# 20 instead of 21 matmuls per feature block of the first FFN products, with the sums on VectorE and the copies on ScalarE

## The chip, the cores and the metric

One core of one Trainium2 chip. The metric is the device time of one execution in microseconds (us), as the median of several. Ratios between kernels are the mean time of one kernel's fast runs over the mean of the other's fast runs of the same rounds, so they are not quite the ratio of the medians quoted beside them. Names in the profile: PE is TensorE (PEld its weight loads), DVE is VectorE, ACT is ScalarE, POOL is GpSimd, SP is SyncE, and SPq is SyncE's queue of DMA issues. PSUM is the memory that the matmuls here write to, SBUF the one that they read from. L511 is line 511 of the kernel in question.

## The reference

```python
# q, k, v: (8, 8, 576, 64); w1, w2, w3: (512, 768); w_out: (768, 512); all computed in fp32
scores = (q @ k.transpose(0, 1, 3, 2)) / sqrt(64)
attn = (scores * Dmat) @ v                    # Dmat: gamma ** (row - col) below the diagonal, else 0
x = attn.transpose(0, 2, 1, 3).reshape(4608, 512)
h = maximum(maximum(x @ w1, x @ w2), x @ w3)  # first products
out = h @ w_out                               # second products
```

## The kernel before

The kernel works in nine tiles of 512 tokens, each of four chunks of 128. The first tile uses plain products while the weights are still being converted. From the second tile on, the first products are bilinear: a unit (one of three weights, two blocks of 128 features, 512 tokens, 512 inputs) is a 2 x 2 x 2 block product made with 7 products instead of 8. Each of the 7 is two matmuls of 128 x 128 by 256 columns, since the inner dimension of a half is 256.

```python
def up(t, h, fp, i):                      # cut
    x = ps_x.tile([P, NH], FP32, ...)     # NH = 256 columns
    product(1, x, True);  p1 = kept("p1", x)      # kept: ScalarE copies x to SBUF
    y = ps_y.tile(...)
    product(2, y, True);  vector.tensor_tensor(c11, y, p1, op=add)
    product(6, x, False); u2 = kept("u2", x)      # adds to the same bank after the copy
    z = ps_y.tile(...)
    product(7, z, True);  p7 = kept("p7", z)
    product(5, x, False); vector.tensor_tensor(c22, x, p7, op=add)
    product(4, z, False); vector.tensor_tensor(c21, z, u2, op=add)
    product(3, x, False)                          # then maxima into h
```

The retention (scores, masks, values, states) of the next tile is done in steps between units. Each step puts its instructions on the engines at once.

```python
opool = ctx.enter_context(tc.tile_pool(name="opool", bufs=2))
def store(r, c, osb, ...):
    nc.sync.dma_start(block..., osb...)           # same queue as all loads
def total(r, c, src, others):
    osb = opool.tile([P, NM, DM // 2], FP32, tag="osb", name="osb")
    for m, o in enumerate(others):
        nc.vector.tensor_tensor(osb[:, m, :], src[m], o[:], op=ALU.add)
    store(r, c, osb)
# retention steps of a pair of chunks a, b; m counts the parts of a tile
at(m, (keep, a), (transposes, a), (load, a + 2))
at(m + 1, (transposes, b), (decay_values, b))
at(m + 2, (scores, a), (scores, b), (load, b + 2))
at(m + 4, (decay_values, a + 2))
at(m + 5, (values, [a, b], [b, a + 2]))
```

## Time and profile before

| | before |
|---|---|
| time, median of 3 runs | 798.76 us (798.38 to 799.25) |
| span of the profiled run | 796.0 us |
| busy: TensorE / VectorE / ScalarE / GpSimd | 785.0 / 417.6 / 174.4 / 139.9 us |
| waits of TensorE on other engines and loads | 7.5 us, 6.2 of them in the first 30 us |
| one steady tile (from first second-product to the next tile's) | 84.4 to 85.3 us, the last 75.7 us (it has less retention) |

The table says that TensorE is the bound and hardly ever waits. The lines, and how they are read, are in the prediction below.

### The profile page before, as it was taken

The page shows a single profiled execution, that of the slowest core. Times are in us where ns is not written, and L with a number is a line of the kernel's source. Part 1 is how long each engine was busy: PE and PEld are TensorE (multiplying, and loading weights), DVE is VectorE, ACT ScalarE, POOL GpSimd, SP SyncE. Part 2 cuts the span into 40 slices and gives each one's busy share as a digit, 9 for nine tenths or more (in the row PEclk, how much of TensorE's full clock was granted, in tenths as well). Part 3 has the DMA queues.
Part 4 walks back from the last instruction along what each step waited for, and adds up shares of the span by engine and source line. Part 5 has one row for each costly group of instructions (what it writes and reads, how often), then busy time and mean ns, then how long its engine had stood idle before and what let it go on. Part 6 is the DMA issues. An engine that isn't in the chain of part 4 may idle for free.

```text
span 796.0 us, 13774 instructions
## 1 busy us (share of the span) xinstructions
PE 785.0 (99%) x5172; PEld 643.0 (81%) x5172; DVE 417.6 (52%) x833; ACT 174.4 (22%) x402; POOL 139.9 (18%) x158
## 2 busy tenths in 40 slices
PE   8899999999999999999999999999999999999998
PEld 7445456888888888888888888888888888888887
DVE  2898979664454534364535354544545343642441
ACT  2664632111111111111111111111111111112111
POOL 3110108511210130112111121112111201110000
DMA  9995643333333323332233423333333332001001
GB/s 212 233 230 127 173 91 100 57 55 57 89 58 57 58 75 61 64 58 60 63 56 55 89 59 57 57 57 90 58 55 57 78 68 54 1 14 40 1 1 53
DMA packets 236930, 59.27 MB, mean 74 GB/s; under 512 B 217920, under 2 KB 235584, under 8 KB 236864
## 3 DMA queue, kind: packets, MB, share of 16 engines
q1 hardware_dynamic: 236432, 58.14, 33.9%
q8 instruction: 40, 0.66, 0.4%
q10 hardware_dynamic: 432, 0.27, 0.1%
q14 instruction: 26, 0.21, 0.1%
HBM read 48.89 MB, written 9.44 MB: 73 GB/s over the span
## 4 chain that ended last, share of the span: by engine, by line
PE 95%; SPq 2%; DMA 1%; issue 0%; ACT 0%; DVE 0%; ACTq 0%
PE x L511 32%; PE z L511 15%; PE dx L383 11%; PE up L573 8%; PE y L511 8%; PE dz L383 5%; PE s L204 4%; PE o L257 4%; PE dy L383 3%; PE down L562 2%; PE o L270 2%; PE kv L224 2%; SPq L172 1%; DMA kraw<-in_k_dram 1%; SPq L327 0%; DMA out_dram<-osb 0%
## 5 line engine op out<-in xcount | busy, mean ns | idle before, releaser
L511 PE MATMUL x<-S,T 128*128 128x256 f32 x576 | 148.0, 379 | 0.6 <-ACT p L516 0.6
L511 PEld LDWEIGHTS x<-S,T 128*128 128x128 f32 x576 | 109.0, 190 | 16.4 <-ACT p L516 1.0
L361 POOL TENSOR_TENSOR H<-h 128x256 f32<-128x256 f32 x24 | 21.0, 873 | 320.9 <-DVE h L554 320.9
L511 PE MATMUL x<-xT,w 128*128 128x256 f32 x288 | 76.1, 387 | 0.0
L511 PE MATMUL x<-S,w 128*128 128x256 f32 x288 | 74.4, 381 | 0.7 <-DVE h L541 0.7
L511 PE MATMUL z<-xT,T 128*128 128x256 f32 x288 | 73.9, 379 | 0.0
L511 PE MATMUL y<-xT,w 128*128 128x256 f32 x288 | 73.9, 379 | 0.0
L511 PE MATMUL z<-S,w 128*128 128x256 f32 x288 | 73.9, 379 | 0.0
L541 DVE TENSOR_TENSOR tmp<-x,p 128x256 f32<-128x256 f32 x48 | 20.4, 425 | 100.2 <-PE x L511 100.2
L516 ACT COPY p<-x 128x256 f32<-128x256 f32 x72 | 26.8, 372 | 192.1 <-PE x L511 192.1
L286 DVE TENSOR_TENSOR xT<-o,gq 128x512 f32<-128x512 f32 (+1 forms) x40 | 23.6, 633 | 84.6 <-PE o L270 84.6
L573 PE MATMUL up<-xT,w 128*128 128x512 f32 x144 | 63.5, 596 | 0.5 <-DVE xT L286 0.5
L511 PEld LDWEIGHTS x<-S,w 128*128 128x128 f32 x288 | 49.4, 189 | 14.2 <-issue 1.3
L511 PEld LDWEIGHTS z<-S,w 128*128 128x128 f32 x288 | 54.7, 190 | 7.4
L511 PEld LDWEIGHTS y<-xT,w 128*128 128x128 f32 x288 | 54.7, 190 | 7.4
L511 PEld LDWEIGHTS x<-xT,w 128*128 128x128 f32 x288 | 53.0, 190 | 9.6 <-issue 1.5
L511 PEld LDWEIGHTS z<-xT,T 128*128 128x128 f32 x288 | 54.2, 189 | 7.9
L573 PEld LDWEIGHTS up<-xT,w 128*128 128x128 f32 x144 | 26.8, 190 | 32.3 <-issue 29.8
L207 DVE TENSOR_TENSOR st<-s,causal 128x512 f32<-128x512 f32 x72 | 45.0, 684 | 11.6 <-PE s L204 10.7
L176 POOL TENSOR_TENSOR vd<-vraw,gk 128x512 f32<-128x512 f32 x36 | 38.8, 1077 | 62.1 <-DMA vraw<-in_v_dram 62.1
L516 ACT COPY u<-x 128x256 f32<-128x256 f32 x72 | 26.8, 372 | 100.1 <-PE x L511 91.7
L383 PE MATMUL dx<-To,H 128*128 128x256 f32 x192 | 44.8, 383 | 0.0
(95 smaller groups left out, 1061.8 us busy)
## 6 DMA issues: line engine op xcount, KB each, us to landing
bits<-in_moe_w_dram SPq DMA_DIRECT2D x36, 256.0 KB, 5.1
out_dram<-osb SPq DMA_DIRECT2D x35, 256.0 KB, 2.1
kraw<-in_k_dram SPq DMA_DIRECT2D x32, 256.0 KB, 3.0
vraw<-in_v_dram SPq DMA_DIRECT2D x32, 256.0 KB, 3.5
qraw<-in_q_dram SPq DMA_DIRECT2D x464, 16.0 KB, 1.8
kxraw<-in_k_dram SPq DMA_DIRECT2D x464, 16.0 KB, 1.8
bits<-in_moe_w_out_dram SPq DMA_DIRECT2D x6, 512.0 KB, 4.5
qraw<-in_q_dram SPq DMA_DIRECT2D x6, 256.0 KB, 4.9
```

Source lines behind the costliest of these rows:

```text
L176: nc.gpsimd.tensor_tensor(t[:], raws.pop(("v", g))[:], gk[:].unsqueeze(2).to_broadcast([C, H, D]), op=ALU.mult)
L204: nc.tensor.matmul(s[j][:, p, :], lhsT=kT[r, p, :], rhs=qT[r, p, :], start=True, stop=True)
L207: nc.vector.tensor_tensor(st[:, j], s[j][:], masks[start_of(g)][:].unsqueeze(1).to_broadcast([C, NP, C]), op=ALU.mult)
L224: nc.tensor.matmul(kvs[g][half(h % 2), h // 2, :], lhsT=kr[r:, h, :], rhs=vds[g][r:, h, :], start=True, stop=True)
L257: nc.tensor.matmul(o[n % 2][half(c), m, n // 2, :], lhsT=vds[g][:, h, :], rhs=sts[g][:, h % 2, h // 2, :], start=m == 0 and n < 2, stop=be ...
L286: nc.vector.tensor_tensor(xT[t][:, b::2, i * C:(i + len(chunks)) * C].rearrange("p u (m c) -> p u m c", c=C), o[b][:].rearrange("p m u c - ...
L361: chores.append(lambda: (pool(s3, a11, a21, op=ALU.subtract), pool(s4, a12, s2, op=ALU.subtract)))
L383: nc.tensor.matmul(out[m], lhsT=hS[n](fp)[:, m * P:(m + 1) * P], rhs=late["T"][n][:, fp, :], start=first and fp == 0 and (m == 0 or last a ...
L511: nc.tensor.matmul(out[:], lhsT=w[:, d * P:(d + 1) * P], rhs=xS[t][n][:, d, :], start=first and d == 0, stop=d == 1, skip_group_check=True)
L516: nc.scalar.copy(c[:], src[:])
L541: nc.vector.tensor_tensor(c22, x[:], p7[:], op=ALU.add)
L573: nc.tensor.matmul(ps[:], lhsT=w_sb[i, fb][:, dc * P:(dc + 1) * P], rhs=xT[t][:, dc, :], start=(dc == 0), stop=(dc == NDC - 1))
```

## The change

The intent: one block of 128 features for all three weights is now made with 20 matmuls of 256 columns, where the 2 x 2 x 2 scheme needs 21. Partial sums build up in five PSUM chains (A to E). ScalarE copies 14 intermediate states of a block into a ring of 20 SBUF buffers, and VectorE joins them with 14 additions and maxima. Sums of x and of the weights all go to VectorE. Retention's VectorE operations and its loads no longer go out at once: they are queued (`soon`), and one is taken after every second product. In the second tile two of six blocks stay plain, to cover the making of the weight sums.

```diff
+PRODUCTS = """E a11 b12, E a14 b42, B s15 n5, A a22 b21, C s3 b23, B s19 b41, A s10 b32, C a13 b31, B s6 n2, A s13 b22,
+              C a11 b11, B s14 n1, A s11 n4, D s7 b43, B a23 n6, A s20 b33, D s16 b13, B a21 n3, A a21 n8, A a24 n7"""
...
-                raws[n, g] = raw.tile([P, NP, C // 32, 32], FP32, tag=n, name=n + "raw", bufs=3 if n == "q" else 2)
+                raws[n, g] = raw.tile([P, NP, C // 32, 32], FP32, tag=n, name=n + "raw", bufs=2)
...
+    def soon(step):
+        if spread:
+            urgent.append(step)
+        else:
+            step()
...
-            s1, s2, s3, s4 = (spool.tile([P, 2, NH], FP32, tag=f"S{n}", name=f"S{n}") for n in (1, 2, 3, 4))
-            nc.vector.tensor_tensor(s1[:], a21, a22, op=ALU.add)
...
+            for n, line in enumerate(X_SUMS):          # 13 sums of x, all on VectorE
+                soon(partial(step, n, *line))
...
+        def after(step):
+            if step not in ("E1", "E2", "C2", "C3", "A6", "B5"):
+                t = of[step] = ppool.tile([P, NH], FP32, tag="part", name="part")
+                nc.scalar.copy(t[:], ps[step[0]][:])
+            for out, ins, op in JOINS.get(step, ()):
...
+            nc.tensor.matmul(ps[chain][:], lhsT=factor(w, fb), rhs=xS[t][x], start=n == 1, stop=ends, ...)
+            after(f"{chain}{n}")
...
+        plain = (2, 3) if t == 1 else ()
...
-            at(m, (keep, a), (transposes, a), (load, a + 2))
-            at(m + 1, (transposes, b), (decay_values, b))
-            at(m + 2, (scores, a), (scores, b), (load, b + 2))
+            at(m, (keep, a), (transposes, b), (decay_values, b))
+            if a == 2 * CPT:
+                at(m, (load, a + 2))
+            at(m, (load, b + 2))
+            at(m + 2, (scores, a), (scores, b))
             at(m + 4, (decay_values, a + 2))
-            at(m + 5, (values, [a, b], [b, a + 2]))
+            at(m + 5, (values, [a, b], [b, a + 2]), (transposes, a + 2), (load, a + 4))
```

The cuts leave out the sums of the weights, the joins' table, the smaller buffer counts for the loads of k and v, and a first warm-up loop that is merged into another.

## The prediction

> **What bounds the kernel now.** I read the page's first table, then TensorE's waits, then a stretch of the timeline, because the sum of waits tells whether anything but TensorE's own work is worth removing.
>
> The page, busy time of each engine and the chain that ended last:
>
> ```profile
> PE 785.0 (99%) x5172; PEld 643.0 (81%) x5172; DVE 417.6 (52%) x833; ACT 174.4 (22%) x402; POOL 139.9 (18%) x158
> ...
> PE 95%; SPq 2%; DMA 1%; issue 0%; ACT 0%; DVE 0%; ACTq 0%
> ```
>
> TensorE (PE) is busy in 785.0 of 796.0 us and carries 95% of the chain. A busy PE need not be a full one, so the waits of its own instructions are needed (us in total, times, longest):
>
> ```profile
> PE kt L194 <- DMA kraw<-in_k_dram: 3.9, 2, 2.7
> PE warm L120 <- POOL ident masks.py:199: 1.4, 1, 1.4
> PE x L511 <- DVE h L541: 0.7, 1, 0.7
> PE x L511 <- ACT p L516: 0.6, 1, 0.6
> ```
>
> All seven rows of its waits come to 7.5 us, 5.3 of them before the first product. So only two things change the time: less TensorE work, or new waits. The price of the work is in the timeline, as start, duration, engine, line:
>
> ```profile
> 402.10 1.03 PE L511 MATMUL x<-xT,w 128*128 128x256 f32 x4
> ...
> 402.96 1.03 PE L511 MATMUL y<-xT,w 128*128 128x256 f32 x4
> 403.16 0.37 ACT L516 COPY p<-x 128x256 f32<-128x256 f32 x1 [3.03 <-PE x L511]
> ...
> 403.61 0.84 PEld L511 LDWEIGHTS x<-S,T 128*128 128x128 f32 x4
> 403.82 1.03 PE L511 MATMUL x<-S,T 128*128 128x256 f32 x4
> ```
>
> Each row is one product of two matmuls, recorded as four passes (every fp32 matmul of the program leaves two records). The reader should take the distance between starts, not the durations: from 400.37 to 413.32 fifteen products take 12.95 us, so a product costs 0.863 us and a 256-column matmul **0.432 us**. For 512 columns the chain of waits has
>
> ```profile
> 79.01 13.74 PE up L573 x32
> ```
>
> 32 passes in 13.74 us, so **0.859 us** per matmul: the plain product pays the same per column, and splitting columns in half is free.
>
> **What the Trainium skill says.** (1) "TensorE: Matmul & The Clock Gate", Back-to-back issue gap, gives N/2.4 + 2.5 ns warm, 109 ns for 256 columns. The pitch here is 216 ns per recorded pass, twice that; I use the trace. (2) "PSUM — Partial Sum Buffer", The four PSUM rules, says a synchronised read in the middle of an accumulation group is allowed, and its Specifications say VectorE may take only one tensor input from PSUM. The rows above agree with the first: ScalarE copies x at 403.16 and the next product adds to the same x at 403.82. Both together are why the change needs ScalarE copies. (3) "SBUF — State Buffer", SBUF: two separate sides, says a VectorE operation with two SBUF inputs and a GpSimd operation that reads SBUF lock each other out of a shared port pair. The trace agrees (mean ns of one):
>
> ```profile
> L295 DVE TENSOR_TENSOR S<-S,xT 128x512 f32<-128x512 f32 x8 | 13.1, 1631 | 0.3
> L294 DVE TENSOR_TENSOR S<-xT 128x512 f32<-128x512 f32 x8 | 5.5, 693 | 0.3
> ```
>
> The same addition takes 1631 ns instead of 693 where GpSimd works on its own S. (4) "Perfetto Trace Analysis", Optimizing Scalar/DVE Operations, says about half of a profiled duration overlaps the next instruction. In part:
>
> ```profile
> 139.10 0.42 DVE L545 TENSOR_TENSOR tmp<-z,u 128x256 f32<-128x256 f32 x1 [0.37 <-PE z L511]
> 139.44 0.41 DVE L547 TENSOR_TENSOR h<-h,tmp 128x256 f32<-128x256 f32 x1
> ...
> 149.12 0.42 DVE L343 TENSOR_TENSOR To<-w_out 128x256 f32<-128x256 f32 x1
> 149.58 0.43 DVE L344 TENSOR_TENSOR To<-w_out,To 128x256 f32<-128x256 f32 x1
> ```
>
> Independent VectorE operations start 0.34 us apart, and one that reads the result just before it starts 0.46 us after it.
>
> **The change part by part.** The order of instructions of both kernels gives exact counts.
>
> TensorE. Before: 8 token tiles x 9 units x 14 = 1008 matmuls of 256 columns. After: 46 blocks of 128 features x 20 = 920, and 24 more plain 512-column matmuls, because the second tile does two of its six blocks plainly while VectorE makes weight sums. Removed: 88 x 0.432 = 38.0 us. Added: 24 x 0.859 = 20.6 us. **Net -17.4 us**, all on the path. Second products (336 matmuls), first tile and retention keep their counts. The two warm-up loops become one; that is before data arrives, and I give it 0. Floor: 798.8 - 17.4 = **781.4 us**. The 2% line is 0.98 x 798.76 = 782.8, so 1.4 us of new waits decides the class.
>
> ScalarE. Before, 216 kept copies plus 24 to h; after, 644 kept copies, 14 per block. At 0.372 us that is 89 us out and 240 in: 174 to about 335 us, 43%. Inside a block 14 x 0.372 = 5.2 us of the 8.6 us that its 20 products take. The critical distance: the order leaves two products (0.863 us) between two steps of chain A or B, the same as now between x and x. In the rows above the copy ends at 403.53, the weight load starts at 403.61 and the matmul at 403.82, so the slack is some 0.1 to 0.2 us if ScalarE starts at once. Copies at most every 0.432 us and lasting 0.37 us keep that, but a late one is felt.
>
> VectorE. Per block 14 joins (before, 9 additions and 8 units of maxima per pair of blocks, 8.5 per block). Per tile 13 sums of x instead of four larger operations, two of them on GpSimd; once, 57 weight sums, all on VectorE. Steady tile, with starts 0.34 to 0.46 us apart (0.60 for 512 elements, 0.62 for transposes, both from the timeline): 84 joins 30, 13 x-sums 5.3, 8 masked scores 4.8, 8 transposes 5.0, 4 xT 2.4, states, H and output sums 6: 54 us, plus some 4 of port lock, of a tile that becomes 84.5 - 2.6 = 82 us. Before, 40.3 of 84.5. Total: 417.6 - 8 x 40.3 = 95 for the first tile, 8 x 58 and 57 x 0.42 = 24, about 580 us or 74%. It is not the bound on average. Block by block, VectorE's work between two E joins against TensorE's time between two E products: first block of a tile 8.6 to 10 us (joins, two late x-sums, four transposes, two states) against 8.6; second 7.5 against 10.6; the others 5.1 to 7.8 against 8.6 to 12.4. The first block runs VectorE 2 to 4 us late, the second takes it back. How late may it be? D's first product needs the bank that the E join frees, and comes 10 products (4.3 us) after B's first; the ring of 20 buffers gives some 4 us too. So these first blocks are near the edge: I add 0 to 0.6 us in each of 7 tiles, and 0.5 to 1 us in the second tile, where weight sums run under plain products.
>
> GpSimd loses 16 sums of x (24.3 us) and 18 of weights (15.6 us): 140 to 100 us. Loads keep their bytes; buffers for later chunks go from 3 to 2 (q, v) and 4 to 3 (k), each refilled as soon as its transposes are done, about half a tile (41 us) ahead, where one chunk's issues take 17 us of the queue. No wait expected.
>
> Sum: 781.4 + 1.6 = **783.0 us**.
>
> **Rivals.** (a) *Nothing waits*: the chains, the ring and the spreading are made for that, and PE waits for ACT or DVE in only four places today. Then 781 to 782. (b) *VectorE becomes a local bound*: a first block of 10 us or more of VectorE work behind x-sums that end late. If it costs 1 us a tile and another 2 in the second tile, 790. Against it: 4 us of tolerance and slack in the next block. (c) *ScalarE's hand-over is too tight*: 0.15 us of slack is used up at every fourth copy; at 0.05 us for each of 644 copies, 32 us, all the gain and more. Against it: the same distance is met 143 times of 144 today. (d) *A late load* after the smaller buffers: some us once per tile; the 24 us of margin speak against it.
>
> **Range and chances.** The floor is firm (counts times pitches, within 1 us), so nothing much below 780. Upwards is open: (b) mild reaches 786 to 790. Time 783.0, range 780 to 790. The centre sits on the 2% line: faster 0.47, same 0.48, slower 0.05 for (c).
>
> **What would show it.** Right: steady tiles of 82 us (81.7 to 82.5), products still 0.432 us apart within a block, PE busy near 767 us, TensorE's waits on VectorE and ScalarE in sum below 4 us, ACT near 335 us and DVE near 580. Rival (b): TensorE waits on a join or ScalarE on VectorE in the first block of each tile. Rival (c): many short waits of A and B on the kept copies, block length above 8.7 us. Rival (d): waits on loads behind transposes. Wrong would be the whole reading if the products' pitch changes when every matmul switches bank, which nothing before shows.

## The result, and the profile after

The changed kernel took **789.01 us** (786.77 to 790.04, 4 runs) against 798.57 us of the kernel before (797.85 to 799.25, 4 runs): ratio 0.9877, 95% interval 0.9852 to 0.9902. That is 1.2% faster and counts as the same at 2%. It lies in the predicted range, near its upper end, 6 us above the predicted time.

The profiled run had a span of 785.1 us. The page, busy time and the chain that ended last:

```profile
PE 770.2 (98%) x5000; PEld 624.6 (80%) x5000; DVE 559.6 (71%) x1248; ACT 326.2 (42%) x808; POOL 100.5 (13%) x124
...
PE 70%; DVE 12%; SPq 10%; DMA 5%; issue 2%; ACT 0%; DVEq 0%; ACTq 0%
```

VectorE's and ScalarE's busy times came near the estimates. What the reader should notice is the second line: TensorE's share of the chain fell from 95% to 70%, and 10% now runs through the queue of DMA issues. The waits of TensorE (total us, times, longest) say where:

```profile
PE s L240 <- DVE qT L177: 3.3, 6, 0.7
PE qt L229 <- DMA qraw<-in_q_dram: 1.9, 2, 1.6
PE warm L147 <- POOL ident masks.py:199: 1.4, 1, 1.4
PE b L579 <- DVE s L344: 1.4, 3, 0.6
```

Two of them are new and recur: six waits of the scores on a transposed q, and waits of chain B on a sum of x. The price of a product is unchanged, as the timeline of TensorE inside a block shows:

```profile
300.17 0.59 PE L579 MATMUL b<-s,n 128*128 128x256 f32 x2
300.60 0.59 PE L579 MATMUL a<-s,n 128*128 128x256 f32 x2
301.03 0.59 PE L579 MATMUL d<-s,w 128*128 128x256 f32 x2
```

Starts are 0.43 us apart, although each matmul here adds to another chain than the one before it. To see where the gain went, cut the run by tiles, at the first matmul of each tile's second products (L383 before, L424 after). Over the seven tiles from 190 us on, the count of products promises 42 blocks x 0.432 = 18.1 us. Before, this part took 584.4 us (190.05 to 774.45), after 573.5 us (189.69 to 763.19): 10.9 us came in. Of the missing 7.2 us, comparing each start with the one before it plus the price of its work gives 4.2 us at the six waits on q (a wait of 0.55 us costs about 0.7, the restart included), 1.9 us at the waits on sums of x that fall in this part, and 1.1 us of small gaps.

VectorE and SyncE's queue around the first products of one tile explain the second kind. Columns are start, duration, engine; the bracket is idle time and what ended it:

```profile
356.29 7.94 SPq L195 DMA_DIRECT2D qraw<-in_q_dram  x16
...
361.38 0.76 DVE L441 TENSOR_TENSOR osb<-dy,part 128x256 f32<-128x256 f32 x2 [1.30 <-PE dy L424]
364.27 8.64 SPq L195 DMA_DIRECT2D kxraw<-in_k_dram  x16
372.78 0.76 DVE L441 TENSOR_TENSOR osb<-dx,part 128x256 f32<-128x256 f32 x2 [10.64 <-PE dx L424]
...
374.12 5.39 SPq L436 DMA_DIRECT2D out_dram<-osb  x4
377.78 0.76 DVE L441 TENSOR_TENSOR osb<-dz,part 128x256 f32<-128x256 f32 x2 [2.26 <-DMA out_dram<-osb]
...
382.19 0.67 PE L579 MATMUL b<-s,n 128*128 128x256 f32 x2 [0.60 <-DVE s L344]
```

The output dy is ready at 362 us, but its store is issued at 374.12, because SyncE's queue is issuing loads until then. The two output buffers are both in use, so VectorE stands still for 2.26 us before the third output sum. Eleven sums of x stand behind it in VectorE's order, and TensorE reaches B's third product before the ninth of them, which that product reads, is done. The kernel before had the beginning of this (same views, the tile at 444.59):

```profile
453.88 0.39 SPq L172 DMA_DIRECT2D kraw<-in_k_dram  x1
454.36 0.53 SPq L172 DMA_DIRECT2D vraw<-in_v_dram  x1
455.01 12.81 SPq L397 DMA_DIRECT2D out_dram<-osb  x4
...
464.19 0.76 DVE L402 TENSOR_TENSOR osb<-dz,u 128x256 f32<-128x256 f32 x2 [0.69 <-PE dz L383]
```

There the first store was issued 10.4 us after the tile's second products began (455.01 - 444.59), and its buffer was free long before dz. After the change it is issued 18.2 us after (374.12 - 355.93). There are no more loads in front of it than before: between the last store of a tile and the first of the next, both kernels issue the loads of four chunks in one row of some 72 us (383.03 to 454.89 before, 302.35 to 374.03 after). What changed is when the row begins. Last stores of the tile before and first loads, before the change and after it, with VectorE's transpose of q:

```profile
370.29 12.69 SPq L397 DMA_DIRECT2D out_dram<-osb  x4
383.03 7.60 SPq L162 DMA_DIRECT2D qraw<-in_q_dram  x16
...
290.81 5.79 SPq L436 DMA_DIRECT2D out_dram<-osb  x4
301.63 0.69 DVE L177 STREAM_TRANSPOSE qT<-qraw 128x512 f32<-128x512 f32 x1
302.35 7.46 SPq L195 DMA_DIRECT2D qraw<-in_q_dram  x16
```

Before, the first load follows the last store within 0.05 us. After, SyncE's queue stands idle for 5.7 to 6.3 us in each of six tiles, until 0.03 us after a transpose that reads a buffer of q; there are two such buffers now and were three. So the row begins 6.1 us later, counted from the start of the second products (29.2 instead of 23.1 us), and the tile is 1.9 us shorter: together about the 7.8 us. That the missing third buffer makes the queue wait is argued from this; no run puts it back.

### The profile page after: what moved, and what is told of

Its sections match the earlier page's. It is cut to its first block, busy times and chain, and to the rows that moved or that the text cites. A ratio compares the mean times of both kernels' runs of the same rounds, so it can differ in the third digit from the quotient of the medians.

```text
span 785.1 us, 14443 instructions
## 1 busy us (share of the span) xinstructions
PE 770.2 (98%) x5000; PEld 624.6 (80%) x5000; DVE 559.6 (71%) x1248; ACT 326.2 (42%) x808; POOL 100.5 (13%) x124
## 4 chain that ended last, share of the span: by engine, by line
PE 70%; DVE 12%; SPq 10%; DMA 5%; issue 2%; ACT 0%; DVEq 0%; ACTq 0%
PE a L579 13%; PE b L579 11%; SPq L195 9%; PE up L600 8%; PE dx L424 7%; PE c L579 6%; PE d L579 4%; PE e L579 3%; PE dz L424 3%; PE o L296 3%; PE s L240 3%; DVE part L559 3%; PE down L589 2%; DMA out_dram<-osb 2%; DVE s L344 2%
## 5 line engine op out<-in xcount | busy, mean ns | idle before, releaser
L559 DVE TENSOR_TENSOR part<-part 128x256 f32<-128x256 f32 x460 | 206.1, 455 | 66.2 <-ACT part L564 58.9
L564 ACT COPY part<-b 128x256 f32<-128x256 f32 x230 | 85.7, 373 | 155.4 <-PE b L579 140.2
L564 ACT COPY part<-a 128x256 f32<-128x256 f32 x276 | 102.8, 373 | 58.7 <-PE a L579 47.9
L579 PE MATMUL b<-s,n 128*128 128x256 f32 x276 | 82.4, 380 | 1.4 <-DVE s L344 1.4
L579 PE MATMUL a<-s,w 128*128 128x256 f32 x276 | 82.2, 379 | 0.0
L579 PEld LDWEIGHTS b<-s,n 128*128 128x128 f32 x276 | 52.0, 190 | 9.9 <-ACT part L564 3.0
L579 PEld LDWEIGHTS a<-s,w 128*128 128x128 f32 x276 | 52.4, 190 | 7.2
L579 PE MATMUL c<-xT,w 128*128 128x256 f32 x184 | 56.6, 389 | 0.0
L579 PE MATMUL d<-s,w 128*128 128x256 f32 x184 | 54.8, 380 | 0.0
L579 PE MATMUL b<-xT,n 128*128 128x256 f32 x184 | 54.7, 379 | 0.0
L424 PE MATMUL dx<-To,H 128*128 128x256 f32 x192 | 44.8, 383 | 0.0
L402 POOL TENSOR_TENSOR H<-h,H 128x256 f32<-128x256 f32 x24 | 18.2, 760 | 188.7 <-DVE H L401 103.6
L424 PEld LDWEIGHTS dx<-To,H 128*128 128x128 f32 x192 | 35.9, 190 | 5.7 <-issue 1.0
```

The costliest lines, as they stand in the source:

```text
L402: urgent.append(lambda: (pool(s3, a11, a21, op=ALU.subtract), pool(s4, a12, s2, op=ALU.subtract)))
L424: nc.tensor.matmul(out[m], lhsT=hS[n](fp)[:, m * P:(m + 1) * P], rhs=late["T"][n][:, fp, :], start=first and fp == 0 and (m == 0 or last a ...
L559: nc.vector.tensor_tensor(out, a, b, op=op)
L564: nc.scalar.copy(t[:], ps[step[0]][:])
L579: nc.tensor.matmul(ps[chain][:], lhsT=factor(w, fb), rhs=xS[t][x], start=n == 1, stop=ends, skip_group_check=True)
```

## The experiments

Theory A: the scores wait because VectorE, late in the first block of a tile, makes the second chunk's transposes too late. Theory B: the sums of x are late because VectorE's order puts them behind an output sum that waits for a store, which waits for load issues. Rivals: VectorE's lateness is only passed on; the hand-over to ScalarE is too tight; the sums of x are too long a chain anyway; the start decides.

"Steady part" is the stretch of seven tiles defined above, read from the profiled run; 584.4 us before, 573.5 us after. It leaves out the start, which varies from run to run. The runs were made in three groups on three chips, each beside the kernel before: c0 to e3 (kernel before 797.4 us), e4 and e6 to e8 (798.34), e5 and e9 to e11 (799.01). Times of different groups are compared by their ratios.

### The changed kernel again (c0)

> The changed kernel again, as the control of this group on the same chip. Every theory expects 786 to 790 us, its two waits on VectorE as in the first profile: the second pair's scores on the transposed q about 3.3 us in 6 places, the B chain on a late sum of x about 1.4 us in 3 places. It also shows how far the spread of its four first runs (3.3 us, against 1.4 us of the kernel before) repeats, and whether it comes from the start (first plain product at 27.8 us) or from later.

Measured: 790.6 us (786.7 to 791.98, 6 runs) against 797.4 us; ratio 0.9903 (0.9881 to 0.9925). Steady part 573.7 us; waits on q 3.3 us in 6 places, on sums of x 1.7 us in 4. The loss repeats. So does the wide spread: 5.3 us against 2.8 us of the kernel before in the same group. In both groups the profiled run was the fastest of the changed kernel, so the traces show its good case.

### Scores one step later (e1)

```diff
-            at(m + 2, (scores, a), (scores, b))
+            at(m + 3, (scores, a), (scores, b))
```

> Scores of each pair of chunks one step later (about 13 products later in TensorE's order). Theory A (VectorE is late in the first block of a tile, so the transposed q of the second chunk is late for TensorE): the wait of 3.3 us on it goes below 0.5, each tile loses 0.6 to 0.7 us, and the time falls by about 4 us against the unchanged kernel. Rival (lateness is only passed on: VectorE's masked scores then come later too, and a wait of the same size opens at the values or at a join): no change within 1 us. Rival (the loss is the hand-over to ScalarE): no change.

Measured: 787.44 us (787.07 to 788.73, 4 runs), ratio 0.987 (0.9854 to 0.9885); steady part 573.2 us. The waits of TensorE:

```profile
PE b L579 <- DVE s L344: 3.1, 5, 0.7
PE a L579 <- ACT osb L472: 1.6, 2, 0.9
```

The wait on q is gone altogether, as theory A says, but the steady part is only 0.3 us shorter than of the changed kernel (573.5), because waits on sums of x grew to 3.1 us and a new one on ScalarE's output copy appeared. In the traces the rival "passed on" is right for this edit alone: a block's time won in one place was lost at the next one. By the medians of the group the edit gives 3.2 us (790.6 to 787.44), near the 4 us of theory A: the trace of the changed kernel shows its fastest execution, so it has less to win than the median. In the trace, VectorE's waits on stores rose from 8.6 to 10.5 us, with a longest of 3.1.

### Stores from ScalarE's queue (e2)

```diff
-            nc.sync.dma_start(block.rearrange(...)[:, blocks], osb[:, blocks])
+            nc.scalar.dma_start(block.rearrange(...)[:, blocks], osb[:, blocks])
```

> Output stores are issued from ScalarE's queue, so they no longer stand behind 17 us of load issues in SyncE's queue. Theory B (the late sum of x comes from the output sum ahead of it in VectorE's order, which waits up to 2.3 us for a store to free its buffer): VectorE's wait on the stores (8.6 us in 5 places) goes to near 0, TensorE's 1.4 us on sums of x too, and the time falls by 1.5 to 2.5 us. Rival (the thirteen sums of x are simply too long a chain for 7.8 us of second products): the wait of TensorE stays at 1 us or more and the time moves by less than 1 us.

Measured: 785.73 us (784.88 to 786.13, 4 runs), ratio 0.9848 (0.9835 to 0.9862); steady part 571.25 us, 2.3 us less than in the changed kernel's first trace; by medians of the group 4.9 us, more than the 1.5 to 2.5 expected. The first store now goes out 6.2 us after a tile's second products begin. VectorE no longer waits on stores at all, TensorE no longer on sums of x. The wait on q stays (3.9 us in 6 places), so it does not come from the stores. Theory B holds, and the rival of a too long chain of sums falls. The Trainium skill has this edit: "Perfetto Trace Analysis", DMA Optimizations, suggests separate DMA-issuing engines for inputs and outputs. The runs agree: the stores no longer stand behind SyncE's loads.

### Both (e3)

> Both edits. If theories A and B are the whole loss, the waits of TensorE fall to about those of the start and the time falls by 5 to 7 us against the unchanged kernel, to 781.5 to 783.5 us, the floor that the count of matmuls gives. If more than 3 us above 781.4 remains, a third loss is still to be found.

Measured: **779.09 us** (778.25 to 780.01, 4 runs), ratio 0.9767 (0.9752 to 0.9782). Steady part 565.8 us: 18.6 us less than before, where 18.1 were promised. The waits of TensorE are those of the start, all of them:

```profile
PE qt L229 <- DMA qraw<-in_q_dram: 2.3, 4, 1.3
PE kt L229 <- DMA kraw<-in_k_dram: 2.2, 2, 1.9
PE warm L147 <- POOL ident masks.py:199: 1.4, 1, 1.4
PE up L600 <- DVE xT L184: 0.5, 1, 0.5
PE s L240 <- ACT qT L231: 0.2, 1, 0.2
```

Theories A and B are together the whole recurring loss. In the steady part of the traces they give 0.3 and 2.3 us alone and 7.7 us together: each of the two edits is in part hidden as long as the other wait is there. By the medians of the group it is 3.2 and 4.9 us alone and 11.5 together (790.6 to 779.09), so the hidden part is smaller, some 3.4 us, with the median of a kernel in it that spreads over 5.3 us. The expectation, 5 to 7 us and 781.5 to 783.5 us, was too small: the two edits also remove what the slower executions of the changed kernel lose, which no trace shows.

### Sums of x ahead of the output sums (e4)

As e1, with the stores on SyncE's queue again, and this in the second products:

```diff
             if n in (1, 3):
                 yield
+            if n == 3:
+                chore(5)
```

> Scores one step later as in e1, stores again on SyncE's queue, but two xT and three sums of x are put ahead of the output sums in VectorE's order (five steps of the queue taken right after the values). Theory B1 (only VectorE's order matters: the sums of x stand behind an output sum that waits for a store): TensorE's wait on sums of x falls to near 0 although VectorE still waits some 8 us on stores, and the steady part (first second-product start of the second tile to that of the last) is within 1 us of the 565.8 us of e3. Theory B2 (the late stores themselves cost, also through ScalarE's output copies): the wait on ScalarE's output copy (1.6 us in e1) stays and the steady part is 2 us or more longer than in e3.

Measured: 779.39 us (777.6 to 780.47, 5 runs), ratio 0.976 (0.9744 to 0.9776); steady part 566.35 us, 0.5 us more than e3. No wait on sums of x, and none on ScalarE's output copy. B1 holds: in the first six tiles the first store still goes out 14.5 to 16.9 us after the second products begin, and costs nothing once no urgent work stands behind it. That VectorE would still wait some 8 us on them was wrong; it waits 1.1 us, since its output sum now comes later.

### Second tile fully bilinear (e6)

e3 with no plain blocks in the second tile:

```diff
             weight_sums(0)
             weight_sums(2)
+            weight_sums(1)
-        plain = (2, 3) if t == 1 else ()
-        order = (2, 3, 0, 1, 4, 5) if t == 1 else (0, 1, 4, 5, 2, 3)
+        plain = ()
+        order = (0, 1, 4, 5, 2, 3)
```

> e3 with all six blocks of the second tile bilinear, none plain. TensorE's work falls by 24 x 0.859 - 40 x 0.432 = 3.3 us, but the first block then needs the 19 weight sums of its features (about 8 us of VectorE) and 13 sums of x at once, with only 6.9 us of second products to cover them. Expected: TensorE waits 6 to 14 us on weight sums at the start of the second tile, and the time is 3 to 10 us longer than e3's. If the plain blocks are not needed, it is 3 us shorter.

Measured: 812.78 us (810.94 to 814.05, 4 runs), ratio 1.0181 (1.0163 to 1.0199).

```profile
PE e L579 <- DVE w L344: 29.4, 3, 11.9
```

The direction was right and the size was not: by ratio some 33 us more than e3, where 3 to 10 were expected. I counted one wait, and there are three (11.9, 8.0 and 9.5 us), one ahead of each pair of blocks, since sums queued behind products were not finished by the next pair either. From the first plain product to the first second-product it takes 194.7 us against 160.6 in e3; the waits less the 3.3 us of saved work are 26.1 of these 34.1 us. Beside the other 8 us stands a low granted clock: 0.50 from 130 to 140 us, 0.67 from 160 to 170 and 0.62 from 200 to 210, where e3 was granted 1.0; that it accounts for all of them is not shown. The plain blocks pay for themselves.

### Dummy matmuls in the gap at the start (e7)

In some traces TensorE waits up to 3 us for the fifth chunk's k, and a low clock is granted after it: in e1, after a gap of 3.06 us at 21 us, the mean from 25 to 31 us was 0.55, in e3, after gaps of 1.95 and 1.27 us, 0.72. It is no rule: the kernel before waits 2.74 us there and is granted 1.00.

```diff
     values([2], [2])
+    warm(20, ps_x, "x")      # 20 matmuls of 128 columns on the identity
     transposes(4)
```

> e3 with 20 dummy matmuls of 128 columns in the gap at about 21 us in which TensorE waits for the fifth chunk's k. Theory C (in some executions that gap lasts long enough for the clock to be granted at 0.55 to 0.72 until about 31 us, which costs up to 3 us and makes the spread): the granted clock of the profiled run is 1.000, the first plain product starts at 27.5 to 28 us, the median falls by 1 to 2.5 us against e3 (779.1) to about 777, and the spread of its runs is below 1.5 us. Rival (the start is bound by the loads, whatever the clock): no change within 0.5 us.

Measured: 779.88 us (779.09 to 780.37, 4 runs), ratio 0.977 (0.9756 to 0.9784), clock 1.0, 0.999 or better in all runs, but not faster than e3.

```profile
21.54 4.73 PE L147 MATMUL warm<-ident 128*128 128x128 f32 x40
26.10 0.60 PE L229 MATMUL kt<-ident,kraw 128*128 128x128 f32 x4
```

The low clock is gone, but the dummies took 4.6 us, longer than the gap, so this run could not tell what the clock is worth. A later version has 8 (below).

### First warm-up of the kernel before, put back (e8)

e3 with the 4 and 24 small matmuls at the very start instead of 6:

```diff
-    warm(6)
+    warm(4)
+    warm_quarters(6)
```

> e3 with the first warm-up of the kernel before put back (4 and 24 quarter matmuls instead of 6). Theory C puts the lost clock at 21 us, long after it, so: no change within 0.7 us, and the spread as in e3 or the unchanged kernel. Rival (the removed quarters are what costs at the start): the first plain product about 1 us earlier, median 1 to 2 us lower.

Measured: 779.79 us (779.25 to 780.57, 4 runs), ratio 0.9771 (0.9756 to 0.9785). No change: that part of the change is worth nothing, as the prediction took it.

### A 21st product (e5)

e3 with the first E product issued twice (the second overwrites, the result stays right):

```diff
-            nc.tensor.matmul(ps[chain][:], ...)
+            for _ in range(2 if chain == "E" and n == 1 else 1):
+                nc.tensor.matmul(ps[chain][:], ...)
```

> e3 with the first E product issued twice in every block (the second clears and overwrites, so the result stays right): 46 more 256-column matmuls. If TensorE's work alone sets the time in e3, it is 46 x 0.432 = 19.9 us longer, 799 us, level with the kernel before. If VectorE or ScalarE set part of it, the extra 0.43 us per block is partly absorbed and the cost is below 17 us.

Measured: 797.66 us (797.14 to 799.26, 4 runs), ratio 0.999 (0.9974 to 1.0007). Steady part 583.94 us, 18.13 us more than e3; 42 x 0.432 is 18.1. The price of a product is exact and nothing is absorbed: in e3 TensorE alone sets the time. With the 21st product back, the steady part is within 0.5 us of the kernel before (583.94 and 584.4), so the rest of the change, sums, copies and ring, is free there.

### One product between two steps of a chain (e9)

e3 with chain C moved forward:

```diff
-              ... A a22 b21, C s3 b23, B s19 b41, A s10 b32, C a13 b31, B s6 n2, A s13 b22, C a11 b11, B s14 n1, ...
+              ... A a22 b21, C s3 b23, C a13 b31, B s19 b41, A s10 b32, C a11 b11, B s6 n2, A s13 b22, B s14 n1, ...
```

> e3 with the products reordered so that two hand-overs to ScalarE per block (B3 to B4, A3 to A4) have one product between them instead of two. The copy ends 1.0 us after its product's start and a weight load follows, so the next step of B can start at about 1.1 to 1.2 us where 0.86 is wanted: 0.2 to 0.35 us for B in each of 46 blocks, after which A's is met. Expected 9 to 16 us longer than e3, as waits of TensorE on the kept copies. If there is slack that I do not see, below 3 us.

Measured: 825.95 us (825.7 to 827.77, 4 runs), ratio 1.0343 (1.0327 to 1.0358): by ratio some 46 us more than e3, about three times the upper end of what I wrote.

```profile
403.60 0.59 PE L579 MATMUL c<-s,w 128*128 128x256 f32 x2
404.65 0.70 PE L579 MATMUL c<-xT,w 128*128 128x256 f32 x2 [0.46 <-ACT part L564]
405.19 0.59 PE L579 MATMUL b<-s,w 128*128 128x256 f32 x2
...
406.49 0.59 PE L579 MATMUL b<-s,n 128*128 128x256 f32 x2
406.92 0.60 PE L579 MATMUL a<-s,w 128*128 128x256 f32 x2
407.54 0.70 PE L579 MATMUL b<-s,n 128*128 128x256 f32 x2
408.08 0.60 PE L579 MATMUL a<-s,n 128*128 128x256 f32 x2
```

The miss is mine: the edit puts C's first two steps side by side, and C's first is a kept one too, so there is a hand-over with nothing between. But the trace gives the number that was wanted. From a kept step to the next of its chain is 1.05 us at least, from start to start (403.60 to 404.65, 406.49 to 407.54), and the product after a stalled one starts 0.54 us later instead of 0.43. Per block: 1.05 - 0.43 = 0.62, 1.05 - 0.86 = 0.19, and two restarts of 0.11, together 1.03 us; times 46 is 47 us. A tile of e9 is 6.18 us longer than one of e3, which is six times 1.03. In the changed kernel the distance is three starts, 1.30 us, so the slack is 0.25 us, where the prediction had 0.1 to 0.2.

### A ring of 16 (e10)

e3 with `PARTS = 16` instead of 20.

> e3 with 16 buffers instead of 20 in the ring of kept copies. ScalarE then waits for VectorE about four copies (some 2.5 us) earlier. If VectorE's lateness in the first block of a tile is 2 to 3 us, as the trace of the changed kernel shows (E's join of the second block at +2 us), ScalarE's waits on the joins grow several times over and TensorE begins to wait on the kept copies: 3 to 15 us longer. If the ring has room to spare: within 1 us of e3.

Measured: 779.8 us (779.01 to 780.58, 4 runs), ratio 0.976 (0.9745 to 0.9775): no change. ScalarE's waits on joins rise from 10.1 to 18.1 us, and TensorE does not notice. The ring was not near its edge.

### The version that the runs point to (e11)

e3, the sums of x ahead of the output sums as in e4, and 8 dummies in the gap:

```diff
+            if n == 3:
+                chore(5)
...
+    warm(8, ps_x, "x")
```

> The version that the runs point to: scores one step later, stores from ScalarE's queue, three sums of x ahead of the output sums, and 8 dummy matmuls (about 1.9 us) in the gap at 21 us, where 20 of them (4.7 us) outlasted the gap. Expected 777 to 778.5 us, a granted clock of 0.999 or more in all runs, first plain product at 28 us; if the dummies buy nothing, 779 to 779.5 as e3 and e4.

Measured: 779.05 us (778.7 to 779.74, 4 runs), ratio 0.9752 (0.9737 to 0.9766), clock 1.0 in all four. So the clock at the start is mended, and the time is that of e3. The dummies buy nothing. By ratio this version, e3 and e4 cannot be told apart; e3 has two edited lines and is the one to keep. All three are 2.3 to 2.5% faster than the kernel before.

## Why the prediction was right or wrong

The time, 789.0 us, fell in the range of 780 to 790, where the prediction had put rival (b), mild (786 to 790), and not its centre. The class was given as nearly even between same and faster, so that same came is no merit. Of the signs that were to show the reading right, the pitch and the ScalarE time came; steady tiles were 82.7 to 83.9 us instead of 81.7 to 82.5, TensorE was busy 770.2 us instead of about 767, and its waits on VectorE and ScalarE were 6.2 us in sum instead of below 4. So the work was counted right and the waiting was not. Point by point:

- **TensorE's net of 17.4 us** was right. The price held (0.43 us apart), a 21st product costs exactly it, and e3's steady part is 18.6 us shorter for 18.1 promised. The floor was some 1 us too high: beside the kernel before of its own group, e3 is 18.3 us faster (797.4 to 779.09). From the first plain product to the first second-product, that is the first two tiles, it takes 160.6 us against 161.3 before, though 0.7 us more work was counted; among the rest are 1.3 us of waits of the kernel before that e3 has not.
- **VectorE about 580, ScalarE about 335, GpSimd 100 us**: 559.6, 326.2 and 100.5. The ScalarE figure is a slip of the sum: 174 - 89 + 240 is 325, which is what came. VectorE is not the bound on average.
- **First blocks near the edge, "0 to 0.6 us in each of 7 tiles"**: the place was right and the size was not (the second tile's 0.5 to 1 us came as 1.0). Six tiles each lose 0.64 to 0.87 us to the late q, and three lose up to 0.78 more to late sums of x. I looked for the wait at joins and the ring (rival b as written); TensorE waited on neither but for 0.2 us, and a ring of 16 costs nothing. It waited on what the lateness delays next: transposes and sums of x. I had counted how much VectorE has to do and not when each consumer asks for it.
- **"No wait expected" from the loads** is the step that failed. I checked that a load comes in time for its own reader, 41 us ahead (and in the steady part TensorE waits on no load, so rival (d) as written did not come), and did not ask what stands behind the load in the same queue. It is the stores. In each of six tiles the queue waits some 6 us for VectorE's transpose of q before the row of loads can begin (q has two buffers instead of three), and the first store goes out 18.2 us after the start of second products instead of 10.4, which holds VectorE for up to 2.3 us. Moving them to another queue removes it (e2, e3), and so does taking the urgent work out from behind them (e4).
- **The mis-sized term**: 1.6 us for new waits, where the profiled run lost 7.2 us in the steady part. That the median lies about 2 to 4 us above the profiled run of the changed kernel is not explained. The clock at the start has a part at most: among the six repeats, 786.7 us went with 0.999 and 792.0 with 0.995 and 0.996, but 0.4% of 790 us is 3.2 us of the 5.3, and mending the clock in e11 did not shorten e3. The slow executions left no trace. The runs of e1, e2 and e3 spread over 1.7, 1.3 and 1.8 us only, which fits waits that add up differently from run to run; that is argued, not shown.
- **Rival c**, the tight hand-over, costs nothing here: TensorE waits on no kept copy. e9 shows how near it is: 0.25 us.

## What to carry to other kernels

When a change takes work off the bounding engine, list for every other engine and queue what stands *behind* each operation in order, and ask of each wait who is next in line: here an output sum, waiting for a store behind load issues, held sums that TensorE needed. When buffers are cut, ask not only whether a load still comes in time, but when the queue gets to what stands behind it: here it began its loads 6 us later. Two small waits in a row hide each other in part, so try the cures together before judging either: in the traces they gave 0.3 and 2.3 us alone and 7.7 together, by medians 3.2, 4.9 and 11.5. Keep stores off the queue that issues many small loads, and test a suspected price by adding the work back (a 21st product cost 18.1 us of the steady part for 18.1 counted).

## What the Trainium skill lacked or had wrong

- "TensorE: Matmul & The Clock Gate", Back-to-back issue gap, gives no pitch for fp32. "FP8 and Floating Point Precision", TensorE Precision Notes, says four passes; four times 256/2.4 ns is an estimate of 427 ns from these two pages, and the runs show 432 ns per matmul of 256 columns and 859 ns for 512. Only two records per matmul appear in the trace, which no page says.
- No page has the cost of a hand-over within an accumulation group: TensorE writes, ScalarE copies 256 columns, TensorE adds to the same bank. The runs show 1.05 us from start to start at least (copy 0.37 us of it), and a start 0.54 instead of 0.43 us after a stalled one. "PSUM — Partial Sum Buffer" only says that the read is allowed.
- "Perfetto Trace Analysis", DMA Optimizations, recommends separate engines for inputs and outputs especially for loops and control flow. The runs show that it matters without any, and with how little: one chunk's 34 issues hold the queue some 17 us, and when the row of them began 6 us later, the stores behind it came 8 us later and held up VectorE.
